# Block-sparse attention with a mixture of experts: the opening loads in another order, V by chunks, and each end block's rows in a DMA of their own

## The chip, the cores and the metric

One core of a Trainium2 chip. The metric is the device time of one execution in microseconds (us), and before the change the median of 3 runs is 654.19 us (651.63 to 657.99).

## What is computed

Attention with a block mask, and then a layer of experts on its output. Sequences have 768 positions in 24 blocks of 32.

```python
q, k, v: (4, 8, 768, 64) float32          # batch, heads, positions, width
scores = q @ k.T / sqrt(64)
mask = |blk_i - blk_j| <= 1               # the block and its neighbours
     | blk_i in (0, 23) | blk_j in (0, 23)  # first and last block see all and are seen by all
     | blk_j in sampled_blocks[blk_i]     # three drawn blocks for each block of queries
attn = softmax(where(mask, scores, -1e9)) @ v
x = attn.transpose(0, 2, 1, 3).reshape(3072, 512)
e = argmax(x @ w_gate); gate = softmax(x @ w_gate)[e]     # 8 experts
out = gate * (relu(x @ w1[e]) @ w2[e])                    # w1 (8, 512, 1024), w2 (8, 1024, 512)
```

## The kernel before

Attention goes through the four batches one after the other. A batch is cut into six groups of queries; the last one, `GL`, comes first, and holds besides its own 64 queries those of the first and last block. Each group has two steps (`half`), of two pairs of heads each, so there are 48 steps. A step computes scores (L332, transposed: keys on the partitions), turns them into exponentials on ScalarE (L349), multiplies by a mask on VectorE (L355, L359), and one step later multiplies by the values (`attend`, `attend_last`, `product` at L373). `divide` (L438) normalises and writes rows to memory. The experts follow: tokens are gathered by expert and two layers of matmuls run (L1121, L1135).

Three kinds of values take part in a step. Neighbouring blocks are copied from V in SBUF (`place_values`, L529). The drawn blocks are gathered by GpSimd (`fetch_values`, L511) row by row out of `v_d` (`v_rows` in the profile), a copy of V in memory with rows of 8 heads x 65 floats, where the 65th column is 1 and gives the sum of the exponentials. The first and last block come by a DMA of SP out of the same copy (`fetch_ends`, L520), for the first two groups of each batch. All three land in the tile `around`. Drawn keys are copied from SBUF into the tile `kr` (`place_keys`, L542).

The opening, batch 0. Keys and queries of a pair of heads come as 128 rows of 768 floats (`fill_rows`, L144) into one of two places for staging, each for one pair of heads. `turn_rows` (L148) turns them on TensorE and copies them out of PSUM, the first head by ScalarE, the second by VectorE. V comes by heads (`load_v`, L160: 128 x 6 pieces of 256 bytes a head), and `keep_v` (L164) writes it to memory in six chunks of 128 positions. `scores_first` computes the scores of the first and last block's queries against all keys, one pair of heads at a time, and `attend_all` (L390) their products with all six chunks of V. PSUM has three tiles for turns and scores (`lend(lent, ps_s=3)`).

The order on TensorE, VectorE, GpSimd, ScalarE and SP is that of the program, written by hand (L278 to L281). SP issues nearly all DMAs. Its order in the opening is: keys and queries of pairs 0 and 1 (L284), V of heads 0 to 3 (L287), and from `turn_first` keys and queries of pairs 2 and 3 as the staging comes free (L412), V of heads 4 to 7 (L414), all of `keep_v` (L415), and the gating weights (L416). The ends of the first two groups (L1283, L1289) are next, and from step 0 on the keys and queries of batch 1 (`fill_next`, L140). DMAs of SP have their completion semaphores from a ring of eight, so that a DMA also waits until the one eight places ahead of it has landed.

```python
    turn_first(0)
    turn_first(1)
    scores_first(0)
    turn_first(2)
    scores_first(1)
    turn_first(3)
    make_masks(*lists)
    scores_first(2)
    scores_first(3)
    for pr in range(NPR):
        attend_all(0, pr, es[("all", pr)], range(NCH))
```

Of the kernel before, what the change touches and what calls it, by code (L numbers as in the profile page):

```python
# [17 lines left out]
def kernel(  # L18
# [11 lines left out]
    nc = tc.nc  # L30
    P = 128
    B, H, S, D = q.shape
    BLK = 32
    NB = S // BLK
    NR = sampled_blocks.shape[1]
    NCH = S // P
    CW = NCH // 2 * P
    NPR = H // 2
# [37 lines left out]
    wg = const.tile([P, DB, E], F32, name="wg")  # L76
# [25 lines left out]
    VW = D + 1  # L102
# [4 lines left out]
    v_d = [nc.dram_tensor(f"v_rows_{b}", (S, VR), F32, kind="Internal").ap() for b in range(B)]  # L107
# [4 lines left out]
    def held(flat):  # L112
        a, c = NPR * S, 2 * NPR * S
        return (
            flat[:, :a].rearrange("p (r s) -> p r s", r=NPR), flat[:, a:c].rearrange("p (r s) -> p r s", r=NPR),
            flat[:, c : c + NCH * VR].rearrange("p (c w) -> p c w", c=NCH),
        )

    sets = [held(other[:]), held(room[:])]
    sets = [sets[(b + B - 1) % 2] for b in range(B)]  # L120
    at = 2 * NPR * S + NCH * VR
    stage = [[room[:, at + (2 * i + j) * S : at + (2 * i + j + 1) * S] for i in range(2)] for j in range(2)]
# [3 lines left out]
    around = mpool.tile([P, 2, 5, VR], F32, name="around")  # L126
    xk = mpool.tile([P, 2, NPR, P], F32, name="xk")
    kr = mpool.tile([P, 2, 2, NPR, NKR], F32, name="kr")
# [12 lines left out]

    KG = S // D

    def fill_rows(b, pr, which, slot):  # L144

        nc.sync.dma_start(stage[which][slot], (k, q)[which][b, 2 * pr : 2 * pr + 2].rearrange("h (i j) d -> (h i) (j d)", j=KG))

    def turn_rows(b, pr, which, slot):  # L148
        src = stage[which][slot]
        tp = upper["ps_s"].tile([P, 2, 512], F32, name="tp", tag="s")  # L150
        for hh in range(2):
            r = slice(hh * D, (hh + 1) * D)
            for j in range(KG // 2):
                nc.tensor.transpose(tp[:, hh, j * D : (j + 1) * D], src[r, j * P : (j + 1) * P], ident[r, r])
        for hh, copy in enumerate((nc.scalar.copy, nc.vector.tensor_copy)):
            to = sets[b][which][hh * D : (hh + 1) * D, pr, :].rearrange("p (i j a) -> p a i j", j=KG // 2, a=2)
            for a in range(2):
                copy(to[:, a], tp[a * D : (a + 1) * D, hh, : KG // 2 * D].rearrange("p (j i) -> p i j", i=D))

    def load_v(b, hs=None):  # L160
        for h in range(H) if hs is None else hs:
            nc.sync.dma_start(sets[b][2][:, :, h * VW : h * VW + D], v[b, h].rearrange("(c p) d -> p c d", p=P))

    def keep_v(b, cs=None):  # L164
        for c in range(NCH) if cs is None else cs:
            nc.sync.dma_start(v_d[b][c * P : (c + 1) * P, :], sets[b][2][:, c, :])
# [114 lines left out]
    attn_by_hand.enter_context(tc.manual_schedule(engines={mybir.EngineType.Activation, mybir.EngineType.SP}))  # L281
    for two in (sets[0][2], sets[1][2]):
        nc.gpsimd.memset(two.rearrange("p c (h w) -> p c h w", w=VW)[:, :, :, D], 1.0)
    for pr in range(2):  # L284
        for which in range(2):
            fill_rows(0, pr, which, pr)
    load_v(0, range(4))  # L287
    make_lists_pool = ExitStack()
    lists = make_lists(make_lists_pool.enter_context(tc.tile_pool(name="mk", bufs=1)))
    rt = {}  # L290
# [6 lines left out]
    def parity(b, g):  # L297
        return (b * NG + order.index(g)) % 2
# [105 lines left out]


    def turn_first(pr):

        for which in range(2):
            turn_rows(0, pr, which, pr % 2)
        if pr + 2 < NPR:  # L410
            for which in range(2):
                fill_rows(0, pr + 2, which, pr)  # L412
        if pr == 1:
            load_v(0, range(4, H))  # L414
            keep_v(0)  # L415
            nc.sync.dma_start(wg[:], moe_w_gate.rearrange("(c p) e -> p c e", p=P))  # L416

    def scores_first(pr):
        (es[("all", pr)],) = scores(plan_all(0, pr))
# [7 lines that stand above are left out]
# [93 lines left out]
    def fetch_ends(b, g):  # L520

        if order.index(g) < 2:
            nc.sync.dma_start(around[:D, parity(b, g), 0, :], v_d[b].rearrange("(n i) w -> n i w", i=BLK)[:: NB - 1])

    def not_before(at):

# [103 lines left out]
    def attention_again():  # L630
        oh, pen = dense_tables(small)
        for b in range(B):
            for two in (sets[b][2],):
                nc.gpsimd.memset(two.rearrange("p c (h w) -> p c h w", w=VW)[:, :, :, D], 1.0)
            load_v(b)
            for pr in range(NPR):
                for which in range(2):
                    fill_stage(b, pr, which)
                    turn(b, pr, which)()
            for g in range(NG):  # L640
                for pr in range(NPR):
                    shifted(b, g, pr, oh, pen)
                    if pr % 2:
                        divide(b, g, pr // 2)
                turn_out(b, g)
                logits(b, g)
            gate(b)
            gate_weights()
# [617 lines left out]
    def early(i):  # L1266
# [13 lines left out]
        if i == 8:  # L1280
            tokens("A", TA, KA)

    fetch_ends(0, GL)  # L1283
    fetch_values(0, GL, 0, 1)
    fetch_values(0, GL, 0, 0)
    place_keys(0, GL, 0)
    place_middle(0, GL)
    place_values(0, GL)
    fetch_ends(0, 0)  # L1289
    V_AT = [  # L1290
        {2: (0,), 3: (1, 2), 4: (3,), 5: (4, 5), 6: (6, 7)}, {0: (0, 1), 1: (2, 3), 2: (4,), 4: (5,), 6: (6, 7)},
# [6 lines left out]
    for i, (b, g, half) in enumerate(steps):  # L1298
# [66 lines left out]
        if half == 0 and nxt is not None:  # L1365
            if i >= 2:
                fetch_ends(*nxt[:2])
                b_, g_, half_ = steps[i - 1]
                not_before(sums[0:1, b_ * NG + g_, 4 * half_ : 4 * half_ + 1])
            fetch_values(*nxt[:2], 0, 0)  # L1370
# [190 lines left out]
```

## Time and profile before

| what | value |
|---|---|
| median of 3 runs | 654.19 us (651.63 to 657.99) |
| profiled execution, its span | 664.23 us, 662.5 us |
| TensorE busy, matmuls | 628.4 us (95%), 8952 |
| VectorE, ScalarE, GpSimd busy | 305.1, 223.7, 182.8 us |
| mean granted TensorE clock | 0.961 |
| first key load issued, first turn | 0.82 us, 6.48 us |
| V's copy to memory issued | 19.51 to 23.46 us |
| products with all chunks of V (L373, 96 matmul instructions) | 22.99 to 29.07 us |
| scores of step 0 begin | 28.99 us |

A page's times are from the start of the span. A row of a timeline has the start, the duration, the engine, the line, the operation, the tiles (out<-in) and the number of instructions, and in brackets the idle time before it and what ended it. PEld is TensorE's loading of weights; SPq and POOLq are issues of DMAs. A float32 matmul counts as two instructions. q1 is the DMA queue of SP and ScalarE, q0 that of GpSimd.

### The profile page before, as it was taken

How to read it: one execution, taken by the hardware profiler on the slowest of the kernel's cores; microseconds unless marked ns; L12 is line 12 of the kernel's file. 1: busy time of each engine (PE TensorE's matmuls, PEld its weight loads, DVE VectorE, ACT ScalarE, POOL GpSimd, SP SyncE). 2: the span in 40 equal slices, each digit the busy share in tenths (PEclk: the TensorE clock that was granted, in tenths of full speed). 3: DMA queues.
4: the chain of work that ended last, by engine and by line, in shares of the span. 5: the costliest groups of instructions: out<-in, count | busy, mean ns of one | idle time of the engine just before them, and what ended most of it. 6: DMA issues, size and time to landing. Idle time of an engine off the chain costs nothing. (4 is left out here: it accounts for less than half of the span.)

```text
span 662.5 us, 21377 instructions
## 1 busy us (share of the span) xinstructions
PE 628.4 (95%) x8952; PEld 524.3 (79%) x8952; DVE 305.1 (46%) x978; ACT 223.7 (34%) x430; POOL 182.8 (28%) x288
## 2 busy tenths in 40 slices
PE   7999999999999998789999999999999999999995
PEld 7888889998999887679776677797769678767962
DVE  6456665774677498632750368200182023702200
ACT  5456756675676554422111011121111111111110
POOL 2146744552354244710111122001300203020210
PEclk7769999999999996969999999999999999999998
DMA  9579966996787237954788999959996699989950
GB/s 266 168 189 231 250 181 157 217 264 171 172 199 218 81 98 267 308 189 165 263 315 303 352 348 347 342 206 361 400 398 245 209 405 395 343 286 391 396 205 19
DMA packets 124857, 170.93 MB, mean 258 GB/s; under 512 B 71028, under 2 KB 71029, under 8 KB 124726
## 3 DMA queue, kind: packets, MB, share of 16 engines
q1 hardware_dynamic: 114688, 137.61, 63.4%
q0 software_dynamic: 10000, 31.59, 14.7%
q8 instruction: 80, 1.31, 0.8%
q14 instruction: 51, 0.42, 0.2%
q10 hardware_dynamic: 38, 0.00, 0.0%
HBM read 150.11 MB, written 19.33 MB: 256 GB/s over the span
## 5 line engine op out<-in xcount | busy, mean ns | idle before, releaser
L1121 PEld LDWEIGHTS hp<-around,room 128*128 128x128 f32 x1216 | 138.4, 192 | 8.3 <-issue 5.6
L1121 PE MATMUL hp<-around,room 128*128 128x128 f32 x1216 | 141.3, 276 | 2.0 <-ACT kr L1128 1.7
L1102 DVE STREAM_TRANSPOSE around<-xg 32x128 f32<-32x128 f32 x208 | 62.9, 302 | 126.1 <-PE hp L1121 95.9
L349 ACT ACTIVATE ea<-s 128x768 f32<-128x768 f32 x104 | 81.4, 811 | 104.7 <-PE s L344 70.8
L1135 PE MATMUL zp<-room,kr 128*128 128x512 f32 x256 | 112.7, 594 | 0.0
L515 POOL DMA_INDIRECT around<-v_rows,rows_of x88 | 95.1, 1081 | 62.4 <-issue 23.7
L373 PE MATMUL op<-around,ea 128*64 128x65 f32 x2112 | 92.0, 232 | 6.2 <-DMA around<-v_rows,rows_of 3.4
L373 PEld LDWEIGHTS op<-around,ea 128*64 128x64 f32 x2112 | 79.9, 143 | 14.9 <-issue 6.3
L1135 PEld LDWEIGHTS zp<-room,kr 128*128 128x128 f32 x256 | 47.5, 190 | 54.6 <-issue 54.6
L355 DVE TENSOR_TENSOR ea<-ea,mask 128x768 f32<-128x768 f32 x80 | 74.4, 957 | 20.6 <-ACT ea L349 14.7
L1128 ACT ACTIVATE kr<-hp 128x512 f32<-128x512 f32 x36 | 21.4, 598 | 119.1 <-PE hp L1121 104.9
L1150 POOL DMA_INDIRECT out_dram<-kr,sB x14 | 14.1, 1006 | 164.6 <-ACT kr L1140 106.1
L1140 ACT ACTIVATE kr<-zp,xg 128x512 f32<-128x512 f32 x16 | 11.0, 690 | 100.3 <-PE zp L1135 100.3
L1228 DVE STREAM_TRANSPOSE ea<-ea 32x128 f32<-32x128 f32 x84 | 21.7, 285 | 32.6 <-DMA ea<-x_rows,gB 31.9
L1150 POOL DMA_INDIRECT out_dram<-kr,sA x5 | 5.1, 1020 | 89.8 <-ACT kr L1140 89.8
L344 PE MATMUL s<-other,kr 64*128 64x64 f32 x352 | 29.4, 273 | 0.5 <-issue 0.2
L339 PE MATMUL s<-room 64*64 64x64 f32 x736 | 27.2, 249 | 2.2 <-issue 1.9
L344 PE MATMUL s<-room,kr 64*128 64x64 f32 x352 | 28.5, 267 | 0.7 <-issue 0.5
L344 PEld LDWEIGHTS s<-other,kr 64*128 64x128 f32 x352 | 27.4, 201 | 1.0 <-issue 0.9
L344 PEld LDWEIGHTS s<-room,kr 64*128 64x128 f32 x352 | 26.3, 194 | 1.3 <-issue 1.3
L339 PE MATMUL s<-other 64*64 64x64 f32 x736 | 25.0, 231 | 1.9 <-issue 1.4
L339 PEld LDWEIGHTS s<-room 64*64 64x64 f32 x736 | 22.0, 158 | 4.8 <-issue 3.4
(342 smaller groups left out, 870.7 us busy)
## 6 DMA issues: line engine op xcount, KB each, us to landing
room<-in_moe_w_dram SPq DMA_DIRECT2D x46, 2048.0 KB
room<-in_moe_w_dram SPq DMA_DIRECT2D x16, 512.0 KB
x_rows<-xb SPq DMA_DIRECT2D x20, 256.0 KB
room<-in_k_dram SPq DMA_DIRECT2D x24, 192.0 KB
room<-in_q_dram SPq DMA_DIRECT2D x24, 192.0 KB
v_rows<-room SPq DMA_DIRECT2D x12, 260.0 KB
v_rows<-other SPq DMA_DIRECT2D x12, 260.0 KB
room<-in_v_dram SPq DMA_DIRECT2D x16, 192.0 KB
```

Source lines behind the costliest of these rows:

```text
L339: nc.tensor.matmul(s[j * D : (j + 1) * D, hh, a : a + n], lhsT=keys(r), rhs=queries(r), start=True, stop=True)
L344: nc.tensor.matmul(s[:, hh, a : a + n], lhsT=keys(r), rhs=queries(r), start=True, stop=True)
L349: nc.scalar.activation(e, s[:, :, : 6 * D], AF.Exp, scale=scale)
L355: nc.vector.tensor_tensor(e, e, m[:, None, :].to_broadcast([P, 2, 6 * D]), op=ALU.mult)
L373: nc.tensor.matmul(op[ti * D : (ti + 1) * D, pr % 2, hh, : D + 1], lhsT=e, rhs=values[:, (2 * pr + hh) * VW : (2 * pr + hh + 1) * VW], sta ...
L515: nc.gpsimd.indirect_dma_start(out=around[p0:, par, 1 + ti + 2 * ch, :], out_offset=None, in_=v_d[b][:, :], in_offset=bass.IndirectOffsetO ...
L1102: nc.vector.transpose(xT[d, :, t], xg[t, :DM].rearrange("p (c q) -> p c q", c=DB)[:, :, d])
L1121: nc.tensor.matmul(hp[:, m, :], lhsT=st[i]["w1"][:, c, fb * P : (fb + 1) * P], rhs=st[i]["xT"][:, c, :], start=(c == 0), stop=(c == DB - 1),)
L1128: nc.scalar.activation(hT[:, g * (FB // 2) : (g + 1) * (FB // 2), :], hp[:], AF.Relu)
L1135: nc.tensor.matmul(zp[:], lhsT=st[i]["hT"][:, fb, :], rhs=st[i]["w2"][:, fb, :], start=(fb == 0), stop=(fb == FB - 1),)
L1150: ins = nc.gpsimd.indirect_dma_start(out=to[:, :], out_offset=bass.IndirectOffsetOnAxis(ap=at, axis=0), in_=rows, in_offset=None, bounds_c ...
L1228: nc.vector.transpose(xT_u[d, :, j * P + tq * 32 : j * P + (tq + 1) * 32], xg_u[t, j, :DM].rearrange("p (c q) -> p c q", c=DB)[:, :, d],)
```

## The change

All eight loads of keys and queries of batch 0 are asked for at once; the four of pairs 2 and 3 go into `kr`, the room of the drawn keys, which has just 4 x 768 floats a partition. V comes by chunks of 128 positions with all 8 heads (`load_chunk`, 128 x 8 pieces of 256 bytes), and the copy of chunk c - 2 to memory is issued after the load of chunk c. The gating weights follow. In `fetch_ends` one DMA of two blocks (source [2, 32, 520]) becomes two DMAs of 32 rows, here and at its six later places.

```diff
-    def fill_rows(b, pr, which, slot):
-        nc.sync.dma_start(stage[which][slot], (k, q)[which][b, 2 * pr : 2 * pr + 2].rearrange("h (i j) d -> (h i) (j d)", j=KG))
-    def turn_rows(b, pr, which, slot):
-        src = stage[which][slot]
+    def fill_rows(b, pr, which, to):
+        nc.sync.dma_start(to, (k, q)[which][b, 2 * pr : 2 * pr + 2].rearrange("h (i j) d -> (h i) (j d)", j=KG))
+    def turn_rows(b, pr, which, src):
...
+    def load_chunk(b, c):
+        nc.sync.dma_start(
+            sets[b][2][:, c, :].rearrange("p (h w) -> p h w", w=VW)[:, :, :D], v[b].rearrange("h (c p) d -> c p h d", p=P)[c],
+        )
...
-    for pr in range(2):
-        for which in range(2):
-            fill_rows(0, pr, which, pr)
-    load_v(0, range(4))
+    early_room = kr.rearrange("p a b r w -> p (a b r w)")
+    first = {}
+    for n in range(2 * NPR):
+        pr, which = n // 2, n % 2
+        first[(pr, which)] = stage[which][pr] if pr < 2 else early_room[:, (n - 4) * S : (n - 3) * S]
+        fill_rows(0, pr, which, first[(pr, which)])
+    for c in range(NCH):
+        load_chunk(0, c)
+        if c > 1:
+            keep_v(0, (c - 2,))
+    keep_v(0, (NCH - 2, NCH - 1))
+    nc.sync.dma_start(wg[:], moe_w_gate.rearrange("(c p) e -> p c e", p=P))
...
     def turn_first(pr):
         for which in range(2):
-            turn_rows(0, pr, which, pr % 2)
-        if pr + 2 < NPR:
-            for which in range(2):
-                fill_rows(0, pr + 2, which, pr)
-        if pr == 1:
-            load_v(0, range(4, H))
-            keep_v(0)
-            nc.sync.dma_start(wg[:], moe_w_gate.rearrange("(c p) e -> p c e", p=P))
+            turn_rows(0, pr, which, first[(pr, which)])
...
         if order.index(g) < 2:
-            nc.sync.dma_start(around[:D, parity(b, g), 0, :], v_d[b].rearrange("(n i) w -> n i w", i=BLK)[:: NB - 1])
+            for j in range(2):
+                row = j * (S - BLK)
+                nc.sync.dma_start(around[j * BLK : (j + 1) * BLK, parity(b, g), 0, :], v_d[b][row : row + BLK, :])
```

## The prediction

> **What bounds the kernel now.** I read the page first. In part 1 TensorE is busy 95% of the span, and in part 2 its row is nines nearly everywhere, but the clock row begins 7 7 6:
>
> ```profile
> PE   7999999999999998789999999999999999999995
> PEclk7769999999999996969999999999999999999998
> ```
>
> So the whole is bound by TensorE, and an opening that ends earlier moves everything behind it forward. The change touches the first 30 us and six small loads later, so next I read the waits between 0 and 45 us:
>
> ```profile
> POOL around L515 <- DMA v_rows<-room: 22.0, 1, 22.0
> DVE ea L359 <- issue: 7.5, 1, 7.5
> ACT ea L349 <- remote: 5.3, 1, 5.3
> PE tp L154 <- DVE room L158: 1.7, 1, 1.7
> PE op L373 <- DVE ea L359: 0.7, 1, 0.7
> PE op L373 <- DMA around<-v_rows,rows_of: 0.6, 1, 0.6
> PE tp L154 <- DMA room<-in_k_dram: 0.3, 1, 0.3
> ```
>
> TensorE waits for a key load just once, 0.3 us (exactly 0.26: the turn at 12.57). The 1.7 us before it is a wait for a PSUM buffer to be copied out, which no load shortens. "All loads first" therefore removes 0.26 us and no more. GpSimd's 22 us look large, but nothing of GpSimd's is due before that. What counts is whether its gathers land before TensorE needs them. The timeline of 26.5 to 38 us:
>
> ```profile
> 26.96 1.21 SPq L523 DMA_DIRECT2D around<-v_rows  x2
> 27.81 1.17 POOL L515 DMA_INDIRECT around<-v_rows,rows_of  x1 [22.01 <-DMA v_rows<-room]
> 28.27 4.02 SPq L140 DMA_DIRECT2D room<-in_k_dram  x2
> 29.28 0.93 POOL L515 DMA_INDIRECT around<-v_rows,rows_of  x1 [0.30 <-issue]
> 32.44 0.81 ACT L349 ACTIVATE ea<-s 128x768 f32<-128x768 f32 x1 [5.35 <-remote]
> 34.35 0.70 PE L373 MATMUL op<-around,ea 128*64 128x65 f32 x4 [0.70 <-DVE ea L359]
> 35.61 2.43 PE L373 MATMUL op<-around,ea 128*64 128x65 f32 x20 [0.56 <-DMA around<-v_rows,rows_of]
> ```
>
> V's copy in memory is there at 26.96. The two gathers follow at 27.81 and 29.28 and release TensorE only at 35.61, over 5 us after the second was issued. In the DMA view of 31 to 33 us:
>
> ```profile
> q0 software_dynamic: 105, 0.27, 53.3%
> q1 hardware_dynamic: 36, 0.06, 12.8%
> ```
>
> SP's queue (q1) moves 0.06 MB in 2 us, with two loads of ends and one of keys issued in full and a second of keys held up in its issue (3.6 of the 4.02 us). The same queue moved 375 GB/s at 21 to 23 us. And the stages:
>
> ```profile
> core 0: us, PE busy (x) PEld busy (x) DVE busy (x) ACT busy (x) POOL busy (x), PEclk, DMA share, GB/s
> 36.00:44.00 8.00, 8.00 (x102) 7.65 (x101) 3.81 (x10) 3.15 (x8) 3.13 (x5) 0.50 0.83 199
> 44.10:50.20 6.10, 6.10 (x166) 5.64 (x169) 3.42 (x10) 3.77 (x6) 3.08 (x6) 1.00 0.85 206
> ```
>
> After that starved stretch TensorE runs 10 us at half clock: 12.8 matmuls per us, against 27.2 right after.
>
> **What the Trainium skill says.** "DMA: Bandwidth & Descriptors", section "Why a DMA increments its semaphore by 16 and not by 1": a DMA is spread over the largest number of engines, up to 16, that divides the slowest dimension of both sides. Line 523's source is [2, 32, 520], so its 130 KB go over two engines. The trace agrees: 0.06 MB in 2 us on q1. The same page, "Queues, rings and completion order": each engine takes one queue's descriptors in order and alternates between queues. So what SP issues behind the ends stands behind them on two engines, and the gathers' shares there share those engines; the late release at 35.61 and the 3.6 us issue agree. "TensorE: Matmul & The Clock Gate", Part 1: the clock is halved after a window of about 3.4 us with too little activity, and restored after a busy one; the windows run free of the kernel. The trace has half clock at 10 to 23.6 and from 33.8 to 44.1, each after a gap.
>
> **The change part by part.** All sums are against the profiled execution: 664.23 us, span 662.5, so 1.7 lie around the span. It was 10 us above the median of 654.19; I subtract the saving from the median.
>
> *Keys and queries first.* The eight loads are 3.15 MB. At 341 GB/s (measured at 11 to 14 us) from 2.0 on they are in by 11.2; the third pair's key, waited for at 12.57, well before. Gain 0.26 us. The first two pairs stay first: no change. The drawn keys' room is first written at 23.07 by VectorE; the last turn reads it near 18.4. So the new wait there is over when it is asked, with VectorE's mask multiplications behind it: cost 0, cover 4.6 us.
>
> *V by chunks.* 6 loads of 1024 pieces instead of 8 of 768: the same 6144 pieces, so no gain of rate. At 224 GB/s (15 to 18 us) a 262 KB chunk takes 1.17 us, and a copy to memory (266 KB at 375 GB/s) 0.71. SP's order is c0 c1 c2 k0 c3 k1 c4 k2 c5 k3 k4 k5. From 11.2: c0 12.4, c1 13.6, c2 14.7, k0 15.4, c3 16.6, k1 17.3, c4 18.5, k2 19.2, c5 20.4. A copy waits on SP for its chunk's landing, some 1.3 us after the data (before: data ended at 18.2, the copy was issued at 19.51). Behind that wait stand the next chunk and all later loads. But c1 and c2 are queued ahead and cover 2.3 us. Before, V was in at 18.2; now at 20.4, landed about 21.7. Its first reader is the product with all chunks (L392), at 22.99, now 22.7, which needs c5 only 1 us later: cover about 2 us. k5 is issued at 21.7; before, 3.5 us passed from the last copy's issue end to its landing (23.46 to 26.96). So V's copy is complete near 25.6, 1.3 us earlier. Eight issues of V cost SP 10.6 us with backpressure before; I assume the same total.
>
> *The ends.* Two DMAs of 32 rows each, so 16 engines. The 266 KB take 0.7 us and not the 5 or more they took two engines. It costs two more issues (0.55 us each, median 540 ns) on SP, ahead of the next batch's key loads, which have slack: 25.6 + 2.2 is 27.8 against 28.27. The gathers, issued near 26.5 and 28.0, no longer share two blocked engines. Most of their data was in by 33 even so (q0 moves 0.06 MB from 33 to 36, against 0.27 from 31 to 33); 1.3 us earlier that is below 32. TensorE's wait at 35.61 goes. The later six of these loads are behind a step's slack; I count 0 (bound 0 to 0.5, the longest pause of products on `around` between 44 and 250 us that no DMA ended).
>
> *What is late next.* The mask (L359), after the exponential at 32.44. That one started 1.9 us after its matmuls (ended 30.5), while TensorE itself stood on "issue" between 30.9 and 32.25. Nothing shows the cause. Similar stalls from 277 to 286 (TensorE 4.0 of 9 us busy) and a profiled run 10 us long suggest that they belong to profiling. If the stall stays, the last 20 products start at 34.1 + 0.7 = 34.8 instead of 35.61: 0.8 gained, the 0.26 included. If it is absent in timed runs, TensorE starts at 32.1 and they at 32.6: 3.0. I take 1.9 for both together.
>
> *The clock.* Between 36 and 44 us 102 matmuls took 8.0 us; at the 27.2 per us that follow, 3.75. So up to 4.25 are to be had if the gaps shrink enough that no window is called idle, and 0 if not. I take two of three windows: 2.8. The other engines don't stop it: in those 8 us VectorE is busy 3.8, ScalarE 3.2. But then the next gathers may be late; the longest such wait elsewhere in attention is 1.0. Bound 0 to 1.0; one such wait comes in the 40 steps up to 250 us, so I take 0.1.
>
> Sum: 1.9 + 2.8 - 0.1 = 4.6 us. 654.2 - 4.6 = **649.6**.
>
> **Rivals.** *Wait gone, clock stays half.* The windows run free, and the wait for the mask (0.7) and the stall remain in the same window. For: between 10 and 20 us a busy share of 97% didn't restore it. Gain 1.9, time 652.3. *Nothing moves.* The copy is late after all, or the gathers are slow by themselves; then only 0.26 us: 654. Against: the queue at 12.8%. *Slower: SP's waits starve V.* If each copy's wait isn't covered, a chunk costs its 1.17, the landing 1.3 and the issue 0.5 to 0.7, that is 3 us; three of them in series after c2 bring c5 to 14.7 + 9 = 23.7, landed 25, and with SP's backpressure (single issues of 3.5 us seen) 27. TensorE then stands in the products with all chunks from 24 to 27, the copy is complete at 31, the gathers land at 37, and the half clock (4 us) is prolonged: 3 + 1.5 + 2 makes 660.5. It decides from c5 landing later than 24. Against: two chunks queued ahead.
>
> **How the numbers follow.** Main forecast 0.55, own range 646 to 651.5 (gain from 2.7 to 8: stall absent and full clock, 3.0 + 4.25 + 0.5); half clock stays 0.25; nothing moves 0.12; slower 0.08. The range takes all but the slower case and the outer tail: 646 to 655.5. About 1% (6.5 us) is what a measurement of this kernel can tell from none. Faster by more needs under 647.7: the best 0.22 of the main case's 0.55. Slower by more needs over 660.7: half of the slow case, and some for what I don't see, 0.06. Within: 0.72.
>
> **What would show it.** The turn at 12.57 without its wait. SP's queue near 300 GB/s in the 3 us after the ends are issued, and no key load's issue of 3.5 us there. The first product with `around` (L373) released by the mask and not by a DMA. PEclk 1.00 where 34 to 44 us is now. Wrong if L392's products wait for V, if the ends still leave q1 at 30 GB/s, or if L373 still waits for the gathers.

## The result and the profile after

| | before | after |
|---|---|---|
| median of 13 runs each | 656.21 us (651.63 to 663.95) | 650.67 us (644.26 to 654.55) |
| ratio after / before | | 0.9907, 95% interval 0.988 to 0.9934 |
| profiled execution, its span | 664.23, 662.5 us | 646.61, 644.9 us |
| mean granted TensorE clock of that execution | 0.961 | 0.979 |

The ratio is a gain of 6.1 us (4.3 to 7.9), where 4.6 was forecast. Some executions fall in a slower state, and the ratios here leave them out, so this one is not exactly that of the two medians, which lie 5.5 us apart. The two profiled executions differ by three times the gain, 17.6 us. By the times at which `divide` normalises, 5.3 us of the 17.6 are gained by the fourth step (54.5 against 49.2) and 7.4 by the end of batch 0 (97.0 against 89.6). Some 8 arise between 273 and 300 us, where the profiled execution of before ran at half clock for 13.7 us (279.6 to 293.2) and that of after did not. Every other profile of this document has 3.4 to 17.1 us of half clock near there, that of the same changed kernel in experiment 9 too (13.7), so this part is not the change's. In what follows lines of the kernel after are 12 higher in the steps: products L385, masks L367 and L371, exponentials L361; gathers are L519 and the ends L529.

The rows of TensorE and its clock on the page after. The third slice of the clock (32 to 48 us), a 6 before, is a 9:

```profile
PE   7989899999999989989999999999989999999994
PEclk8799999999999996999999999999999999999999
```

The waits after between 0 and 45 us (what waited, for what; us in total, times, longest):

```profile
POOL around L519 <- DMA around<-v_rows: 20.3, 1, 20.3
ACT ea L361 <- PE s L356: 7.3, 3, 4.8
PE tp L153 <- DVE room L157: 1.2, 1, 1.2
PE op L385 <- DMA around<-v_rows,rows_of: 1.2, 1, 1.2
PE op L385 <- DVE ea L371: 0.5, 1, 0.5
```

No turn waits for a key load any more; the wait for a PSUM buffer stays. The one wait for gathered rows is another one: it lies at 42.9 us and not before the first `around` products. Those are released by the mask. It was close: in the trace the last of the 16 parts in which the second gather lands comes at 33.02 us, and the first matmul instruction that needs it, the fifth of these products, begins at 33.06. The timeline after, 24 to 38 us:

```profile
25.18 2.20 SPq L529 DMA_DIRECT2D around<-v_rows  x3
26.15 1.17 POOL L519 DMA_INDIRECT around<-v_rows,rows_of  x1 [20.34 <-DMA around<-v_rows]
27.47 0.99 SPq L140 DMA_DIRECT2D room<-in_k_dram  x2
30.43 3.06 SPq L140 DMA_DIRECT2D room<-in_k_dram  x2
30.85 0.81 ACT L361 ACTIVATE ea<-s 128x768 f32<-128x768 f32 x1 [4.78 <-PE s L356]
32.77 1.68 PE L385 MATMUL op<-around,ea 128*64 128x65 f32 x24 [0.53 <-DVE ea L371]
```

V's copy is complete and the first gather issued 1.66 us earlier (26.15 against 27.81), the exponential begins at 30.85 instead of 32.44, and all 24 products run in one go from 32.77. The first key loads behind the ends take 0.99 us to issue where they took 4.02; later ones are held up again, 3.06 us. One of the four loads of ends is out of this view: it needs only the first rows of V's copy, and since it is a DMA of its own it was issued at 23.29. And two stages after, from a table by stage (busy us and instructions of PE, PEld, DVE, ACT and POOL, then PEclk, DMA share, GB/s):

```profile
30.00:34.00 4.00, 3.47 (x68) 3.20 (x65) 2.25 (x5) 3.12 (x7) 0.73 (x1) 1.00 1.21 204
34.00:44.00 10.00, 8.89 (x206) 8.10 (x204) 7.09 (x19) 7.44 (x17) 7.36 (x12) 1.00 1.14 237
```

From 34 to 44 us TensorE has its full clock and issues 206 matmul instructions. Before, the same ten microseconds were at half clock, with 107:

```profile
34.00:44.00 10.00, 9.09 (x107) 8.55 (x108) 5.48 (x15) 5.15 (x11) 4.12 (x6) 0.50 0.74 179
```

TensorE runs the same matmuls in both kernels, and but for a few neighbours they begin in the same order, so they can be counted off in the two traces. The instruction that before begins at 29.0 us is begun 0.3 us later in the kernel after, that of 36.0 us 2.7 earlier, that of 44.0 us 6.2 earlier, and that of 50.0 us 4.8 earlier. The stretch with the waits thus gave 3.0 us, and the fuller clock behind it 2.2: it had given 3.5 by 44 us, and 1.4 of that was lost again, most of it in the new wait at 42.9 (1.16 us). In two more profiles of this opening (experiments 9 and 10) the instruction of 50.0 us is begun 4.9 us earlier.

### The profile page after: what moved, and what is told of

It reads as the page before. It is cut to its first block, busy times and chain, and to the rows that moved or that the text cites. A ratio compares the mean times of both kernels' runs of the same rounds, so it can differ in the third digit from the quotient of the medians.

```text
span 644.9 us, 21378 instructions
## 1 busy us (share of the span) xinstructions
PE 610.8 (95%) x8952; PEld 511.5 (79%) x8952; DVE 303.5 (47%) x978; ACT 223.1 (35%) x430; POOL 187.2 (29%) x288
## 5 line engine op out<-in xcount | busy, mean ns | idle before, releaser
L519 POOL DMA_INDIRECT around<-v_rows,rows_of x88 | 96.9, 1101 | 60.9 <-issue 21.8
L361 ACT ACTIVATE ea<-s 128x768 f32<-128x768 f32 x104 | 79.8, 809 | 87.6 <-PE s L356 78.1
L385 PE MATMUL op<-around,ea 128*64 128x65 f32 x2112 | 89.5, 228 | 11.2 <-DMA around<-v_rows,rows_of 10.0
L385 PEld LDWEIGHTS op<-around,ea 128*64 128x64 f32 x2112 | 77.3, 140 | 20.3 <-DMA around<-v_rows,rows_of 11.6
L367 DVE TENSOR_TENSOR ea<-ea,mask 128x768 f32<-128x768 f32 x80 | 73.1, 954 | 13.0 <-ACT ea L361 12.0
L356 PE MATMUL s<-other,kr 64*128 64x64 f32 x352 | 26.7, 266 | 0.3 <-issue 0.3
L356 PE MATMUL s<-room,kr 64*128 64x64 f32 x352 | 25.6, 260 | 1.1 <-issue 1.1
L356 PEld LDWEIGHTS s<-other,kr 64*128 64x128 f32 x352 | 24.7, 195 | 0.0
L356 PEld LDWEIGHTS s<-room,kr 64*128 64x128 f32 x352 | 23.6, 188 | 1.3 <-issue 1.3
L351 PE MATMUL s<-room 64*64 64x64 f32 x736 | 24.3, 247 | 0.3 <-DVE room L157 0.3
L356 PE MATMUL s<-other,xk 64*128 64x128 f32 (+1 forms) x192 | 22.9, 315 | 1.6 <-issue 1.6
L351 PE MATMUL s<-other 64*64 64x64 f32 x736 | 22.4, 227 | 0.4 <-DVE cnA L777 0.4
```

The source lines that it names most:

```text
L351: nc.tensor.matmul(s[j * D : (j + 1) * D, hh, a : a + n], lhsT=keys(r), rhs=queries(r), start=True, stop=True)
L356: nc.tensor.matmul(s[:, hh, a : a + n], lhsT=keys(r), rhs=queries(r), start=True, stop=True)
L361: nc.scalar.activation(e, s[:, :, : 6 * D], AF.Exp, scale=scale)
L367: nc.vector.tensor_tensor(e, e, m[:, None, :].to_broadcast([P, 2, 6 * D]), op=ALU.mult)
L385: nc.tensor.matmul(op[ti * D : (ti + 1) * D, pr % 2, hh, : D + 1], lhsT=e, rhs=values[:, (2 * pr + hh) * VW : (2 * pr + hh + 1) * VW], sta ...
L519: nc.gpsimd.indirect_dma_start(out=around[p0:, par, 1 + ti + 2 * ch, :], out_offset=None, in_=v_d[b][:, :], in_offset=bass.IndirectOffsetO ...
```

## The experiments

Three chips were used, one for experiments 1 to 4, one for 5 to 8 and one for 9 to 12. The kernel before took 655.45, 668.29 and 667.02 us on them, so each kernel is given as a ratio to before on its own chip, with the gain worked out from the ratio. Of the three, the changed kernel itself was timed on the third alone (9); what is said of 5 to 8 against it compares two chips. "Half-clock time" of a run is (1 - mean granted clock) x 2 x span, averaged over the runs that enter a kernel's ratio; for before it is 44.0, 51.9 and 51.9 us on the three.

My theory was narrower than the prediction, whose step on the ends let the split and the earlier copy act together: the ends on two engines make the gathers late, the late gathers make the wait and the half clock, so the split of the ends is the gain. The main rival was that the earlier copy of V does it.

**1. The split alone, on the kernel before.**

```diff
-            nc.sync.dma_start(around[:D, parity(b, g), 0, :], v_d[b].rearrange("(n i) w -> n i w", i=BLK)[:: NB - 1])
+            for j in range(2):
+                row = j * (S - BLK)
+                nc.sync.dma_start(around[j * BLK : (j + 1) * BLK, parity(b, g), 0, :], v_d[b][row : row + BLK, :])
```

> The kernel before, with the ends in two DMAs of 32 rows each at all eight places and nothing else changed. Theory (the ends on two engines held up what stood behind them): nearly the whole gain, 4 to 6 us, is here; the first product with around is released by the mask, and no half clock follows at 34 us. Rival (V's copy had to be ready earlier): the copy is still complete at 27, so the gathers are still late and the gain is below 2 us.

Measured: 0.9969 (0.9942 to 0.9996), 2.0 us gained. Its timeline:

```profile
27.85 1.17 POOL L515 DMA_INDIRECT around<-v_rows,rows_of  x1 [22.04 <-DMA v_rows<-room]
28.28 0.99 SPq L140 DMA_DIRECT2D room<-in_k_dram  x2
33.27 0.45 PE L373 MATMUL op<-around,ea 128*64 128x65 f32 x4 [0.53 <-DVE ea L359]
34.76 1.80 PE L373 MATMUL op<-around,ea 128*64 128x65 f32 x20 [1.04 <-DMA around<-v_rows,rows_of]
```

SP's queue is freed (the key loads' issue is 0.99 us here too), but the gathers start as late as before and still hold TensorE for 1.04 us; a half clock of 3.4 us follows at 35.5. Over the runs half-clock time hardly falls, from 44.0 to 42.3 us. The theory that the split is nearly the whole gain falls.

**2. The loads alone: the kernel after with the ends in one DMA again.** The diff is that of 1, reversed.

> The changed kernel with the ends again in one DMA of two blocks: keys, queries and V in the new order alone. Theory: the two blocked engines are back, the gathers land after 34 us, half clock follows, and the time is within 1.5 us of the kernel before. Rival (the earlier copy is what counts): it keeps 3 us or more of the gain.

Measured: 0.9954 (0.9932 to 0.9977), 3.0 us gained. Its timeline:

```profile
26.28 1.17 POOL L519 DMA_INDIRECT around<-v_rows,rows_of  x1 [20.49 <-DMA v_rows<-room]
27.69 9.84 SPq L140 DMA_DIRECT2D room<-in_q_dram  x2
34.63 2.43 PE L385 MATMUL op<-around,ea 128*64 128x65 f32 x20 [1.73 <-DMA around<-v_rows,rows_of]
```

The gathers are issued as early as in the kernel after and yet release the products only at 34.63: over 6.8 us after the second issue (27.76). Half clock from 32.2 for 6.8 us. The two key loads right behind the ends take 0.98 us to issue, no more than with the split; the next two loads, queries, hold up SP for 9.84 us.

The trace settles what joint ends do to the gathers. A gather lands in 16 parts, each with its time in the trace. For the second gather of the opening (times in us; the last column is the time from the first issue of keys behind the ends to the end of the fourth issue):

| kernel | ends | issued | 14 of 16 parts landed | all landed | four loads behind the ends |
|---|---|---|---|---|---|
| before | joint | 29.28 | 32.94 | 35.56 | 9.6 |
| 1 | split | 29.32 | 34.61 | 34.71 | 2.2 |
| 2 | joint | 27.76 | 33.11 | 34.58 | 10.9 |
| after | split | 27.63 | 32.62 | 33.02 | 2.9 |

With joint ends two of the 16 parts are 1.3 to 2.6 us behind the others, and the products wait for these two; with the split they are not. The split has a price: in 1 the other fourteen land 1.7 us later than in before, now that the loads behind the ends run beside them. So each half removes one cause of the late gathers, and the other remains. The gains add up within their intervals: 2.0 + 3.0 = 5.0 against 6.1.

**3. The split for the two loads of the opening only, on before.**

```diff
+            if b == 0:
+                for j in range(2):
+                    row = j * (S - BLK)
+                    nc.sync.dma_start(around[j * BLK : (j + 1) * BLK, parity(b, g), 0, :], v_d[b][row : row + BLK, :])
+            else:
...
```

> The kernel before, with the ends in two DMAs only in the first batch (the two in the opening); the six later ones as before. Theory: the later ones stand behind a step's slack, so this is within 1 us of the run with all eight split. Rival (the later ones hold up gathers as well, a part of the gain that the prediction put at 0): 1.5 us or more slower than the run with all eight split.

Measured: 0.997 (0.9945 to 0.9995), the same as with all eight split. The later six are worth nothing that can be seen. In its profiled execution (659.07 us, its median is 654.08) the products waited 5.9 us for the gathers in spite of the split: the gathers were issued at 29.28 and 30.75, and in each of them one of the 16 parts landed 3.0 us behind the others. Nothing in the edit explains that one part.

**4. The clock alone.** The kernel before, with 40 matmuls whose result is not read, between the scores of step 1 and the first `around` products. They keep TensorE busy through the wait and shorten nothing.

```diff
+        if i == 1:
+            fill = upper["ps_s"].tile([P, 2, 512], F32, name="fill", tag="s")
+            for n in range(40):
+                nc.tensor.matmul(fill[:D, 0, :D], lhsT=sets[0][0][:D, 0, :D], rhs=sets[0][1][:D, 0, :D], start=True, stop=True)
```

> The kernel before, with 40 more matmuls of 64 x 64 (80 instructions, some 2.6 us) that nobody reads, between the scores of step 1 and the first product with around, where TensorE waits for the gathers. Theory (the clock is lost because TensorE idles there): no half clock from 34 to 44 us and a time 1 to 4 us below the kernel before although it does more. Rival (the half clock has another cause, or costs nothing because loads bound those steps): half clock as before, and a time equal to before or up to 2.6 us longer.

Measured: 0.9926 (0.9889 to 0.9964), 4.9 us gained (2.4 to 7.3), and half-clock time 36.2 instead of 44.0 us. From its timeline, and from its table by stage:

```profile
29.18 1.17 POOL L515 DMA_INDIRECT around<-v_rows,rows_of  x1 [23.39 <-DMA v_rows<-room]
32.78 4.88 PE L1338 MATMUL fill<-room 64*64 64x64 f32 x80
37.58 1.09 PE L373 MATMUL op<-around,ea 128*64 128x65 f32 x15
```

```profile
34.00:44.00 10.00, 9.44 (x183) 8.99 (x185) 4.42 (x11) 4.22 (x10) 4.74 (x6) 1.00 0.73 172
```

The products start right behind the filler, two microseconds later than in before (37.58 against 35.61), and still the kernel is faster in the timed runs. The filler shortens no wait, which leaves the clock as what it can gain by, and in its profile the ten microseconds behind run at full clock. How much of the 4.9 us lies there is not shown: counted in matmuls without the filler's, this one profile gains 1.7 us on that of before between 29 and 50 us.

**5. Control: the same 40 unread matmuls in the kernel after**, where no gap is left to fill.

> The changed kernel with the same 40 matmuls that nobody reads in the same place. Control for the fourth run. Theory (matmuls put there helped before only because a half clock followed the wait): the changed kernel has little wait and no half clock there, so now they cost time, 0.5 to 3 us over the changed kernel, and half-clock time does not fall. Rival (dense matmuls anywhere in the opening are worth time): 1 us or more below the changed kernel.

Measured: 0.997 (0.9942 to 0.9998). Against the 0.9906 that the kernel after reaches on another chip (9) the matmuls cost about 4.3 us, more than the 3 at most that was expected and near the 4.88 us that they take in the profile. If that ratio holds on this chip too, what 4 gained was no effect of added work as such.

**6. V by heads again, the copy at its end; keys first and the split kept.**

```diff
-    for c in range(NCH):
-        load_chunk(0, c)
-        if c > 1:
-            keep_v(0, (c - 2,))
-    keep_v(0, (NCH - 2, NCH - 1))
+    load_v(0)
+    keep_v(0)
```

> The changed kernel with V by heads as before (8 loads, then the whole copy to memory), but after all keys and queries, and with the ends split. Theory (the earlier copy, and with it the gathers that reach TensorE in time, comes from V by chunks; keys first give 0.3 us): the copy is complete at 26 or later, so the time is within 1 us of the run with the ends alone, some 2 us below the kernel before. Rival (having keys and queries in first is what helps, by letting the opening run through): within 1 us of the changed kernel.

Measured: 0.9966 (0.9943 to 0.9989), 2.3 us gained, against 2.0 of the split alone on another chip. So keys first is worth nothing that these intervals can show, and V by chunks is the part of the loads that counts. Its waits between 0 and 45 us:

```profile
ACT ea L358 <- remote: 5.1, 1, 5.1
PE op L382 <- DMA around<-v_rows,rows_of: 3.4, 1, 3.4
```

The gathers are issued at 27.73 and 29.20 and are waited for again. Of the 3.4 us, 1.8 are due to one of the 16 parts of the second gather, which landed at 36.34 when the other fifteen were in by 34.52; even these were later than the 32.97 at which TensorE began to wait. The half clock, 6.8 us from 32.8, began just before this wait. The first line is the stall ahead of the exponential that before showed and after did not.

**7. The kernel after with 25 unread matmuls in the gap of TensorE near 9 us**, put behind the second pair's turns, to keep the half clock off that begins at 10.6.

> The changed kernel with 25 matmuls of 64 x 64 that nobody reads (1.65 us) where TensorE waits for a PSUM buffer at 8 to 10 us. If that gap starts the half clock of the opening (3.4 to 14 us of it in the profiles so far), the clock falls later or comes back earlier: 5 us less half-clock time and 1 to 3 us less in all. If turns and small matmuls do not count as activity anyway, the half clock is as before and the time is equal within 1 us.

Measured: 0.9957 (0.9932 to 0.9982). The half clock was not kept off: it came at 18.6 for 10.2 us, where the profile of the kernel after has it at 10.6 for 13.7. That it came later need not be the filler's doing, since the profiles of 2, 6, 10 and 12 have it from 18.6 to 19.4 without one. The filler takes 3.12 us, where the gap in the profile of the kernel after is 1.24. If 0.9906 holds on this chip, it cost 3.4 us net. A miss.

**8. The kernel after with three groups of 20, 14 and 30 unread matmuls in the last batch**, where half clock begins near 243 us and TensorE stands near 276.

> The changed kernel with 20 + 14 and 30 matmuls of 64 x 64 that nobody reads where TensorE waits in the last batch, near 240 to 243 and near 276 us (gaps of 1.3, 1.1 and 2.3 us in its profile; every profile so far has a half clock of 10 us after the first two). Theory (gaps of over 1 us make a window idle): that half clock goes or is shorter, and the time is 2 to 4 us below the changed kernel. Rival (those steps are bound by VectorE and loads): the clock is full but the time is the same or up to 2 us longer.

Measured: 0.9971 (0.9947 to 0.9994). Half-clock time fell to 35.1 us, against 51.9 of before on this chip, and still only 1.9 us are gained, less than by the kernel after on the third chip (6.3). The first two groups take 2.54 and 1.84 us in its timeline, ahead of and behind transposes where the kernel after had gaps of 1.32 and 1.05 us, and the third (3.71 us) is longer than either. Less half clock is no gain if more is paid for it on the path.

**9. The kernel after again, on the third chip.**

> The changed kernel itself, beside the kernel before on one chip together with the next three. Theory: 0.6 to 1.2% below the kernel before, as in its own measurement (0.93%), and some 10 us less half-clock time. Rival (the gain hangs on the chip, since on the chip of the last four runs three of its variants stood only 0.3 to 0.4% below): 0.5% or less.

Measured: 0.9906 (0.9874 to 0.9938), 660.50 us, 6.3 us gained: the gain stands on a chip where before takes 667.02. Half-clock time 36.6 against 51.9 us. In its profile too the first `around` products are released by the mask, but 3.4 us of half clock remain there, from 32.1.

**10. The kernel after with the later six ends joint.** The diff is that of 3, in the kernel after.

> The changed kernel with the ends split only in the first batch, and the six later ones in one DMA of two blocks as before. Theory (the prediction's 0 for the later six): within 1 us of the changed kernel on the same chip. Rival: 1.5 us or more slower, since the blocked engines hold up gathers of later batches.

Measured: 0.9911 (0.9875 to 0.9948), 660.76 us, the same as 9. With 3 it says that the six are worth nothing that these intervals can show. Its opening is that of the kernel after, and yet its profile has a wait for the gathers, with 3.4 us of half clock from 32.5:

```profile
32.82 2.43 PE L385 MATMUL op<-around,ea 128*64 128x65 f32 x20 [0.66 <-DMA around<-v_rows,rows_of]
```

The products were ready earlier here (the first four start at 31.71), and the gather was complete at 32.77. So the change brings the gathers in earlier, but not always ahead of the products. In 12, whose opening is the same too, the wait is 0.91 us.

**11. One filler, for the first of these gaps only.** The kernel after with 18 unread matmuls ahead of the transposes L468 of one group of the last batch, where TensorE waits 1.3 us for VectorE near 240 us.

```diff
+    fills = {(B - 1, order[1]): (18, 0)}
...
+            for _ in range(n):
+                nc.tensor.matmul(xr[:D, 1, P : P + D], lhsT=kq[:, :D], rhs=kq[:, D : 2 * D], start=True, stop=True)
```

> The changed kernel with only 18 matmuls of 64 x 64 that nobody reads (some 1.2 us) in the gap of 1.3 us near 240 us. Theory (the half clock of 10 us after it needs that gap, and the longer filler cost as much as it gave by going beyond the gaps): no half clock from 243 to 253 us and 1 to 4 us below the changed kernel on the same chip. Rival: the half clock stays because of the second gap of 1.1 us, and the time is equal or up to 1 us longer.

Measured: 0.9877 (0.9847 to 0.9906), 658.42 us, 8.2 us below before; the lowest ratio here. The filler takes 2.31 us, one more than the gap. From the tables by stage, the kernel of 11 and then that of 9:

```profile
246.00:258.00 12.00, 10.49 (x247) 9.18 (x247) 10.33 (x35) 5.99 (x13) 6.47 (x9) 1.00 0.88 284
```

```profile
246.00:258.00 12.00, 11.50 (x224) 10.80 (x226) 10.00 (x34) 4.75 (x11) 5.29 (x9) 0.72 0.82 266
```

The half clock there is gone, with 23 more matmul instructions in the 12 us (a few of them the filler's last). Against 9 on the same chip it is 2.1 us, but the intervals overlap; that it beats the kernel after is likely and not shown.

**12. Can the gathers' later waits be had?** In the kernel after, keys and queries of batches 1 to 3 come in rows of 3072 bytes as those of batch 0 do, instead of in pieces of 256, and are turned with four copies out of PSUM for each load, two of them on VectorE.

```diff
-        fill_stage(b, n // 2, n % 2, n // 2 % 2)
+        fill_rows(b, n // 2, n % 2, stage[n % 2][n // 2 % 2])
...
-                copy_turned = turn(b + 1, (here - 2) // 2, here % 2, None, (here - 2) // 2 % 2)
+                copy_turned = turn_rows(b + 1, (here - 2) // 2, here % 2, stage[here % 2][(here - 2) // 2 % 2], True)
```

> The changed kernel with keys and queries of batches 1 to 3 loaded in rows of 3072 bytes, as in batch 0, instead of pieces of 256 bytes, and turned as in batch 0 (four copies out of PSUM for a turn, two of them on VectorE, instead of one on ScalarE). Theory (the waits for gathers left in the changed kernel, 10 us in its profile from 44 to 300, come from engines busy with small pieces): those waits fall below 5 us and the time is 1 to 4 us below the changed kernel. Rival (the added copies, 1.2 us of VectorE a turn, bind): 1 us or more slower.

Measured: 1.0078 (1.0056 to 1.01), 5.2 us slower than before and 11.2 slower than 9. The stretch from 44 to 230 us in 9 and then in 12:

```profile
44.00:230.00 186.00, 180.35 (x4858) 166.29 (x4858) 120.34 (x343) 120.78 (x236) 88.53 (x161) 1.00 0.76 192
```

```profile
44.00:230.00 186.00, 175.09 (x4627) 161.00 (x4626) 138.89 (x373) 120.06 (x246) 93.07 (x157) 0.99 0.69 189
```

VectorE is busy 18.6 us more and TensorE gets 231 matmul instructions fewer done. The waits of products for gathers from 44 to 300 us were 2.3 us in 9 and are 1.5 here, so there was little to be had on this chip, and the copies cost far more.

## Why the prediction was right, and where it was not

**Keys and queries first, 0.26 us: right.** The wait at 12.57 is gone, the PSUM wait stays at 1.2 us, and 6 against 1 leaves 0.3 us for this part.

**V by chunks: right in its times, wrong in its worth.** SP's waits did not starve V: no product with all chunks waited for it, so the slower rival did not come. The ends that wait for the whole copy were issued at 25.18, where I had it complete near 25.6, and the gather at 26.15 was forecast near 26.5. But I gave the earlier copy no worth of its own; the loads alone gave 3.0 us, and without the chunks the gain falls to 2.3.

**The ends: right in mechanism, and both edits needed.** My step said that the gathers, issued earlier and no longer sharing two blocked engines, would be in time. Without the earlier copy they were not (1, 6), and with the earlier copy but joint ends they weren't either (2); that the split alone would do nearly all was the error of my first expectation. The spread over more engines that I took from the Trainium skill ("DMA: Bandwidth & Descriptors", "Why a DMA increments its semaphore by 16 and not by 1") agrees with the trace: with joint ends two of a gather's 16 parts land late, and four loads behind the ends take 9.6 and 10.9 us to issue, against 2.2 to 3.4 in 1, 6, 9, 10 and the kernel after. I also forecast SP's queue near 300 GB/s in the 3 us behind. The DMA view of the kernel after, 27 to 30 us, says 0.30 MB, that is 100 GB/s:

```profile
q1 hardware_dynamic: 758, 0.30, 42.8%
q0 software_dynamic: 80, 0.27, 29.8%
```

That is over three times the 0.03 MB per us of 31 to 33 us before, but the loads in it come in pieces of 256 bytes, and I had compared it with a copy in long rows. The gathers came in all the same, at 33.02 with 0.04 us to spare.

**The wait, 1.9 us: within its bounds.** In the profiled executions the last 20 products start 2.5 us earlier (35.61 against 33.06), between the 0.8 and the 3.0 that I had given. It was the case for which I had 3.0: the stall was absent.

**The clock, 2.8 us: near in size, less sure in cause.** Counted in matmuls, the fuller clock from 36 to 50 us gave 2.2, 2.4 and 2.2 us in the profiles of after, 9 and 10. I took two of three windows as saved: in after all three were, in 9 and 10 one of 3.4 us stayed. At full clock I had 3.75 us for what took 8.0 from 36 to 44; in after it took 4.4. With the wait, the three profiles are 4.8 to 4.9 us ahead at 50 us, where I had 4.6 in all. Both terms were middles between two cases, so that the sum came so near is in part luck.

The 6.1 of the timed runs may hold more of the clock: half-clock time is 15.3 us less on the third chip, more than the 10.2 of this stretch. Over the runs of before one us of it goes with 0.28 to 0.34 us of time on the three chips, over those of the kernel after with 0.18; that would make 2.8 to 5.2 us, an estimate from a correlation. Experiment 4 shows by itself that a fuller clock is worth time here, 4.9 us net (2.4 to 7.3).

What starts the half clock is not shown to be the wait for the gathers. In the profile of before it began at 33.82, and the products stood for the gathers from 35.05 to 35.61; ahead of it lie the pauses of the stall (0.38 and 0.50 us) and the beginning of the wait for the mask (from 33.65). In 9 it began at 32.11 without any wait for gathers. The rival "wait gone, clock stays half" would have given 1.9, which is near what the split alone gives (1), and is outside the measured 4.3 to 7.9.

**What is late next, 0.1 us: not settled.** In the profiled execution after, products wait for gathers 10.0 us between 44 and 300 us:

```profile
PE op L385 <- DMA around<-v_rows,rows_of: 10.0, 11, 2.3
```

The first of them, 1.16 us at 42.9, took back part of what the clock had given. But 9 is the same kernel with 2.3 us, and 4, with the loads of before, has 9.3; the four profiles of the first chip have 5.4 to 9.3, those of the other two 1.5 to 4.6. The waits thus go with the execution or the chip more than with the change. What they cost in the median is open.

**The stall, "they belong to profiling": not supported.** Ahead of the exponential it is absent after and in 1, 2 and 4, and there again in 6. The slow stretch near 280 us has half clock in every profile but that of after, and TensorE is busy 4.0 to 9.0 of the 9 us from 277 to 286 there. Both go with chip or execution. A profile is taken in all of them, so profiling alone is not the cause. What is, stays open.

## What to carry to other kernels

Short waits of TensorE are to be priced with the clock behind them: here the fuller clock gave 2.2 to 2.4 us in the stretch behind waits that had cost up to 3.0, and a filler of matmuls in the gap was worth 4.9 us in timed runs, while fillers where no gap was left or well beyond it (5, 7, 8) gave less than the kernel after does without them on another chip. When a gather is late, look both at when it could be issued and at what stands on its engines; here each of two edits took away one cause, and with both the wait was gone in some profiles (after, 8, 9, 11), and 0.66 and 0.91 us were left of it in others (10, 12). An execution that is profiled can be 10 us from the median; compare stage by stage, and the same kernel on other chips, before its differences are put down to a change.

## What the runs showed of the hardware that was not expected

- Half clock came in stretches of 3.4, 6.8, 10.2 and 13.7 us, and once of 17.1 (5), in all kernels, which is multiples of the 3.4 us window of the Trainium skill ("TensorE: Matmul & The Clock Gate", Part 1). Gaps of 1.3 and 1.05 us within 3.5 us (239.6 to 243.1 in the kernel after) stood ahead of one, and with the first of them filled it did not come (11). But one began in 9 at 32.11 with no gap over 0.25 us in the 3.3 us before, TensorE being busy 2.90 of the 3.41 us, so long gaps are not needed.
- The half clock of the opening began between 9.5 and 19.4 us and lasted 3.4 to 13.7 us, with no order by kernel: the same opening had 10.6 for 13.7 us (after), 11.6 for 10.2 (9) and 18.8 for 3.4 (10). A filler at 9 us did not keep it off (7). What starts it was not found.
- Two loads of 130 KB, each with two blocks as its outer dimension, held up the issue of the four loads behind them on SP: 10.9 us for the four (2), against 2.9 with 32 rows to a load (the kernel after).
- Three chips took 655.45, 668.29 and 667.02 us for the same kernel before, while the ratio of after to before was 0.9907 and 0.9906 in two sets of runs.
